# Linear attention with a two-layer feed-forward: seven products over pairs of chunks, with half of the middle results in DRAM

## The chip, the cores and the metric

The kernel runs on one core of a Trainium2 chip. The metric is device time in microseconds (us); the time of a kernel is the median of its runs.

## What is computed

```python
q_s = exp(q - max(q, axis=-1)); q_s = q_s / (sum(q_s, axis=-1) + 1e-9)   # q, k, v: 8 x 8 x 576 x 64
k_s = exp(k - max(k, axis=2));  k_s = k_s / (sum(k_s, axis=2) + 1e-9)
kv = einsum('bhsd,bhse->bhde', k_s, v)
x = einsum('bhsd,bhde->bhse', q_s, kv)        # as tokens: 4608 x 512
h = x @ w_in                                  # 512 x 2048
g = where(h >= 1, h, where(h <= -1, 0, (h + 1) ** 2 / 4))
out = g @ w_out                               # 2048 x 512
```

All is float32. Each large product is made of three matmuls over a high and a low part of its operands (high x low, high x high, low x high).

## The kernel before

The 4608 tokens are nine chunks (0 to 8) of T = 512. For each chunk, `attention(c, pr)` makes x in four pairs of heads: k's maximum (L693 to 696 on VectorE, L733 across partitions on GpSimd), subtraction L737, exponential L742, kv L752; q's softmax (L839 on GpSimd); the product x L896. The feed-forward then runs over NF = 16 blocks f of 128 middle columns. Its second layer is line L1330: for each f, four groups o of 3 matmuls of 512 columns into four PSUM banks o0 to o3, kept over all f.

The first layer has two forms. Chunks 0 to 2 (`PLAIN = 3`) use 12 matmuls h of 512 columns per f (L1169). Chunks 3 to 8 use seven products in place of eight (`PRODUCTS`, `two_first_layers`, L1226) over a 2 x 2 split: two f by the two halves of the chunk's 512 tokens. Each product is 6 matmuls of 256 columns; they build up in the banks hA, hb and hC, with copies sn (L364) and additions (L1250) between them, and leave four results of 128 x 256, which are those of f and f + 1 for all 512 tokens. Sums of weights are made in chunks 1 and 2 (`again`, L528 to L568), kept in DRAM and streamed back for each pair of f (`stream`). The sums of x are made once per chunk in xc (L931) and split into high and low parts (L937, L945).

After the first layer come, per f of 512 tokens: r (L1305, L1308 on ACT), the minimum (L1311 on VectorE), gh (L1315 on ACT) and gl (L1319 on VectorE). Then o can run. All of these have 128 x 512 elements.

The order of work on each engine is made by a planner. `Plan.op` records an operation with its engine, estimated duration, due time and the operations it needs; `Ring` says when a buffer comes free; `order` lists the operations by start and due times; `settle` improves the first part of that list by a search. The list is then issued as it stands, so each engine works through its own in order and a waiting instruction holds up all that stands behind it on its engine. SP issues every DMA.

## Time and profile before

| | |
|---|---|
| runs | 868.08, 863.57, 862.73 us; median 863.57 |
| profiled execution | 868.35 us, of which span 866.2 |
| TensorE (PE) | busy 850.4 us (98%), 5256 matmul instructions |
| VectorE (DVE) | 606.9 us (70%) |
| ScalarE (ACT) | 493.2 us (57%) |
| GpSimd (POOL) | 153.7 us (18%) |
| DMA | 179.09 MB, mean 207 GB/s |

The profile shows one execution. Busy time of an engine is the union of its instructions' spans. The chain is the work that ended last, followed back from the last instruction to what released each step. A row of a group reads: line, engine, operation, output <- inputs, shape, count | busy time, mean ns of one | idle time of the engine ahead of them and what ended it.

### The profile page before, as it was taken

The page shows a single profiled execution, that of the slowest core. Times are in us where ns is not written, and L with a number is a line of the kernel's source. Part 1 is how long each engine was busy: PE and PEld are TensorE (multiplying, and loading weights), DVE is VectorE, ACT ScalarE, POOL GpSimd, SP SyncE. Part 2 cuts the span into 40 slices and gives each one's busy share as a digit, 9 for nine tenths or more (in the row PEclk, how much of TensorE's full clock was granted, in tenths as well). Part 3 has the DMA queues.
Part 4 walks back from the last instruction along what each step waited for, and adds up shares of the span by engine and source line. Part 5 has one row for each costly group of instructions (what it writes and reads, how often), then busy time and mean ns, then how long its engine had stood idle before and what let it go on. Part 6 is the DMA issues. An engine that isn't in the chain of part 4 may idle for free.

```text
span 866.2 us, 14457 instructions
## 1 busy us (share of the span) xinstructions
PE 850.4 (98%) x5256; PEld 733.5 (85%) x5256; DVE 606.9 (70%) x1369; ACT 493.2 (57%) x909; POOL 153.7 (18%) x148
## 2 busy tenths in 40 slices
PE   8999899999999999999899999999999999999998
PEld 6788788888888888888788889889888888888886
DVE  7877777858777788887677787877676764343332
ACT  7887765544556465565456654566554564454444
POOL 5555442111113111112010111110111100000000
PEclk9999999999999999999999999999999999999999
DMA  9989776644755577655656475556554354445431
GB/s 329 292 284 303 252 255 225 213 142 162 247 187 171 194 257 265 217 184 194 222 183 226 175 264 183 212 184 233 198 194 176 133 203 179 177 165 209 183 146 48
DMA packets 47447, 179.09 MB, mean 207 GB/s; under 512 B 5265, under 2 KB 5521, under 8 KB 41233
## 3 DMA queue, kind: packets, MB, share of 16 engines
q1 hardware_dynamic: 47376, 178.18, 58.6%
q8 instruction: 41, 0.67, 0.3%
q14 instruction: 30, 0.24, 0.1%
HBM read 151.95 MB, written 26.21 MB: 206 GB/s over the span
## 4 chain that ended last, share of the span: by engine, by line
PE 89%; DMA 5%; DVE 3%; ACT 1%; issue 1%; POOL 0%; DVEq 0%; POOLq 0%; ACTq 0%
PE o L1330 42%; PE hA L1226 16%; PE h L1169 13%; PE hC L1226 8%; PE hb L1226 4%; PE x L896 3%; DMA st<-in_w 2%; PE kv L752 2%; DMA out<-osb 2%; PE warm L1469 1%; DMA k<-in_kt 1%; DVE hC L1250 1%; DVE st L438 0%; DVE st L441 0%; PE ep L713 0%
## 5 line engine op out<-in xcount | busy, mean ns | idle before, releaser
L1330 PE MATMUL o<-wl,gh 128*128 128x512 f32 x576 | 227.9, 396 | 1.4 <-DVE osb L366 1.3
L1330 PE MATMUL o<-wh,gh 128*128 128x512 f32 x576 | 225.9, 392 | 0.0
L1330 PE MATMUL o<-wh,gl 128*128 128x512 f32 x576 | 225.1, 391 | 0.1
L1226 PE MATMUL hA<-x,w 128*128 128x256 f32 x1152 | 173.6, 287 | 0.9 <-DVE hA L1250 0.5
L1226 PEld LDWEIGHTS hA<-x,w 128*128 128x128 f32 x1152 | 155.5, 190 | 19.4 <-DVE hA L1250 11.1
L1169 PE MATMUL h<-x,w 128*128 128x512 f32 x576 | 144.1, 395 | 0.3 <-DVE x L920 0.3
L1330 PEld LDWEIGHTS o<-wh,gl 128*128 128x128 f32 x576 | 108.3, 188 | 25.1 <-DVE gl L1319 1.3
L1169 PEld LDWEIGHTS h<-x,w 128*128 128x128 f32 x576 | 108.0, 189 | 23.7 <-DVE x L920 1.0
L1330 PEld LDWEIGHTS o<-wl,gh 128*128 128x128 f32 x576 | 108.7, 189 | 19.9 <-DVE osb L366 2.4
L1330 PEld LDWEIGHTS o<-wh,gh 128*128 128x128 f32 x576 | 108.8, 189 | 15.1
L1308 ACT ACTIVATE r<-r 128x512 f32<-128x512 f32 x144 | 91.4, 635 | 3.5
L1226 PE MATMUL hC<-x,w 128*128 128x256 f32 x576 | 85.7, 285 | 3.4 <-DVE gl L1319 3.4
L364 ACT COPY sn<-hA 128x256 f32<-128x256 f32 x87 | 32.5, 373 | 97.6 <-PE hA L1226 97.6
L1226 PEld LDWEIGHTS hC<-x,w 128*128 128x128 f32 x576 | 76.0, 192 | 3.8 <-DVE gl L1319 3.6
L1250 DVE TENSOR_TENSOR hC<-hb,sn 128x256 f32<-128x256 f32 x48 | 20.8, 432 | 81.3 <-PE hC L1226 80.5
L839 POOL TENSOR_TENSOR q<-q,qrz 128x512 f32<-128x512 f32 x36 | 38.2, 1063 | 199.1 <-DVE qrz L861 69.4
L1305 ACT ACTIVATE r<-h,half 128x512 f32<-128x512 f32 x48 | 33.1, 689 | 63.1 <-PE h L1169 62.8
L1305 ACT ACTIVATE r<-hC,half 128x512 f32<-128x512 f32 x48 | 33.1, 690 | 57.3 <-DVE hC L1250 57.3
L1311 DVE SCALAR_TENSOR_TENSOR h<-h,r 128x512 f32<-128x512 f32 x48 | 33.4, 697 | 35.0 <-ACT r L1308 34.7
L839 POOL TENSOR_TENSOR q<-q,qm 128x512 f32<-128x512 f32 x36 | 39.7, 1107 | 75.2 <-DVE qm L819 32.5
L733 POOL PARTITION_ALL_REDUCE m<-m x24 | 18.2, 760 | 195.5 <-DVE m L696 81.1
L1305 ACT ACTIVATE r<-hA,half 128x512 f32<-128x512 f32 x48 | 33.1, 690 | 22.3 <-PE hA L1226 20.1
...
## 6 DMA issues: line engine op xcount, KB each, us to landing
...
q<-in_q SPq DMA_DIRECT2D x36, 256.0 KB, 3.3
out<-osb SPq DMA_DIRECT2D x35, 256.0 KB, 3.9
```

Of the source, the lines that this page charges most:

```text
L364: nc.scalar.copy(out, src)
L733: nc.gpsimd.partition_all_reduce(t["mb"], t["m1"], P, bass_isa.ReduceOp.max)
L752: nc.tensor.matmul(t["kv"][d, :], t["k"][r, j, d], t["v"][r, j, i * (D + 1) : (i + 1) * (D + 1)], start=(j == 0), stop=(j == KJ - 1), tile ...
L839: nc.gpsimd.tensor_tensor(t["qf"], t["qf"], at, alu)
L896: nc.tensor.matmul(t["x"][:, :, p0:p1], lhs, rhs[:, :, p0:p1], start=(i == 0), stop=(i == 2),)
L1169: nc.tensor.matmul(t["h"], lhs, rhs, start=(at == 0 and i == 0), stop=(at == NPAIR - 1 and i == 2),)
L1226: nc.tensor.matmul(where(b), lhs, rhs, start=(begins and not kk and not m), stop=(ends and kk == 1 and m == 2), skip_group_check=True,)
L1250: nc.vector.tensor_tensor(out(), a(), b(), ALU.add)
L1305: nc.scalar.activation(t["r"], t["h"], AF.Relu, bias=half[:, :1], scale=0.5)
L1308: nc.scalar.activation(t["r"], t["r"], AF.Square)
L1311: nc.vector.scalar_tensor_tensor(t["h"], t["h"], 1.0, t["r"], ALU.max, ALU.min)
L1330: nc.tensor.matmul(outs[c, j], lhs[:, s], rhs, start=(f == 0 and i == 0), stop=(f == NF - 1 and i == 2),)
```

## The change

The seven products now go over pairs of chunks, (3, 4), (5, 6) and (7, 8): the 2 x 2 split is two f by two chunks, and each product is 6 matmuls of 512 columns. x of these chunks is written to DRAM (`xo`, `xkept`) and read back into xc, where `x_sums` makes the sums; the high and low parts lie in 14 places x0 to x13, of which chunks 0, 1 and 2 use x0 to x3, x4 to x7 and x10 to x13. The first chunk of a pair goes through the second layer between the products, as before. The second chunk's g (c12 and c22) goes through one of `NGS = 3` rooms gs to DRAM (`keep`), and is read back (`recall`) after the last products of the pair, when 16 f of o alone are run. Weights and their sums share `NWS = 5` rooms. The low parts of x and of a kept g, and the sums, can run on GpSimd or VectorE; `RELUCTANT = 3.0` is added to GpSimd's estimate when the planner chooses. For chunks 2 to 4 (`KM = 5`) k's maximum across partitions is made by a TensorE transpose, a VectorE reduction and a second transpose that spreads it, into the PSUM bank a.

```diff
-    ("P1", "A", 0, A11, B11),
-    ("P2", "B", 0, A12, B21),
-    ("P5", "C", 0, S1, T1),
-    ("P6", "A", 1, S2, T2),
-    ("P3", "C", 0, S4, B22),
-    ("P7", "A", 1, S3, T3),
-    ("P4", "A", 1, A22, T4),
+    ("P1", "A", "B11"),
+    ("P2", "B", "B21"),
+    ("P5", "C", "T1"),
+    ("P6", "A", "T2"),
+    ("P3", "C", "B22"),
+    ("P7", "A", "T3"),
+    ("P4", "A", "T4"),
...
+NWS, NGS = 5, 3
...
+KM = 5
...
-                        w[0] == e or t + us <= start(w[0], op, w[2]) + w[1]
+                        w[0] == e
+                        or t + us + self.bias(op, e) <= start(w[0], op, w[2]) + w[1] + self.bias(op, w[0])
...
                 km = do("DVE", 1.0, 0, k_max, lk, *rm.wait(), port=True)
                 rm.take(km)
 
-                mb = do("POOL", 13.6, 0.1, k_all, km, made[NF - 1, 1])
-                ks = do("DVE", 0.81, 2.5, k_sub, mb, port=True)
-                rm.free(ks)
+                if c < KM:
+                    rb = room("ps a", 1)
+                    tr = do("PE", 0.25, 0.5, k_tr, km, *rb.wait())
+                    rb.take(tr)
+                    kx = do("DVE", 0.25, 1, k_top, tr)
+                    rm.free(kx)
+                    mb = do("PE", 0.25, 1.5, k_spread, kx)
+                    ks = do("DVE", 0.81, 2.5, k_sub, mb)
+                    rb.free(ks)
+                else:
+                    mb = do("POOL", 13.6, 0.1, k_all, km, made[NF - 1, 1])
+                    ks = do("DVE", 0.81, 2.5, k_sub, mb, port=True)
+                    rm.free(ks)
...
-        rxc = room("xc", 1)
-        xo = do("ACT", 0.59, 5, x_out, xm, *(() if hi_half else rxc.wait()), other=[("DVE", 0.69, False)])
+        rxo = room("xo", 1)
+        xo = do("ACT", 0.59, 5, x_out, xm, *rxo.wait(), other=[("DVE", 0.69, False)])
+        rxo.take(xo)
         freed.free(xo)
...
-        xdone[c, kk] = done
+        xkept[c, pr] = dp.tile([P, T], F32, name=f"xk{c}_{pr}")
+        xdone[c, pr] = plan.save(0.45, at(5.2), x_store, [xo], 256)
+        rxo.free(xdone[c, pr])
...
+        for at, (cc, pr) in enumerate(((c, lo), (c + 1, lo), (c + 1, hi), (c, hi))):
+
+            def load(at=at, cc=cc, pr=pr):
+                if not at:
+                    t["xc"] = rp.tile([P, 5, T], F32, tag="xc", name=f"xc_{c}_{kk}", bufs=1)
+                nc.sync.dma_start(t["xc"][:, at, :], xkept[cc, pr])
...
+        def split(part, at, *deps):
+            place = 2 * PARTS.index(part) + kk
+            rx = ring(f"x{place}", 1)
...
+            def high():
+                xs[c, kk, part] = x_room(place)
+                nc.scalar.copy(xs[c, kk, part][:, 0, :], t["xc"][:, at, :])
+
+            def low(engine):
+                eng = nc.vector if engine == "DVE" else nc.gpsimd
+                x = xs[c, kk, part]
+                eng.tensor_tensor(x[:, 1, :], t["xc"][:, at, :], f32(x[:, 0, :]), ALU.subtract)
+
+            h = op("ACT", 0.59, due, high, [*deps, *rx.wait()])
+            rx.take(h)
+            done = either(0.69, low, h)
+            xdone[c, kk, part] = done
+            dones.append(done)
+            return done
...
+        b11 = split("B11", 0, loads[0])
+        t1 = either(0.69, comb(4, 1, 0), loads[0], loads[1])
+        t3 = either(0.69, comb(1, 2, 1), loads[2], t1)
+        t1s = split("T1", 4, t1)
+        b22 = split("B22", 2, loads[2])
+        t2 = either(0.69, comb(0, 2, 4), loads[2], t1, b11)
+        b21 = split("B21", 3, loads[3])
+        split("T3", 1, t3)
+        split("T2", 0, t2)
+        t4 = either(0.69, comb(3, 3, 0), t2, b21)
+        split("T4", 3, t4)
+        rxc.free(*dones)
...
+        def spilled(t, name):
+            def tile():
+                t["h"] = rp.tile([P, T], F32, tag="gs", name=f"{name}_{n}", bufs=NGS)
+                return t["h"]
+
+            return tile
...
+            deps = [loads[k // 2], xdone[c, 0, part], xdone[c, 1, part], *deps]
+            return op("PE", 1.36, due, product(k, begins, ends), deps)
...
-        c11 = dve(c_lo, lambda: where("B"), lambda: side["P1"], due + 0.6, p2, k1, p3)
-        rb.free(c11)
-        c12 = dve(c_hi, c_hi, lambda: side["U2"], due + 0.6, p3, u2)
-        p7 = mm(5, due + 1.0, u2, p6)
-        c22 = dve(a_hi, a_lo, lambda: side["P5"], due + 1.0, p7, k5)
-        rs.free(c11, c12, c22)
-        p4 = mm(6, due + 1.5, c22, p7)
...
+        c11 = dve(h["B"], h["B"], lambda: side["P1"], due + 2.8, p2, k1)
...
+        o12 = dve(spilled(c12, "c12"), h["C"], lambda: side["U2"], due + 8.4, p3, u2, *rgs.wait())
+        rgs.take(o12)
+        rc.free(o12)
+        rs.free(c11, o12)
+        p7 = mm(5, due + 10, u2, p6)
+        o22 = dve(spilled(c22, "c22"), h["A"], lambda: side["P5"], due + 11.4, p7, k5, *rgs.wait())
+        rgs.take(o22)
+        rs.free(o22)
+        p4 = mm(6, due + 12, o22, p7)
+        for mm_ in (p2, p6, p7, p4):
+            rws.free(mm_)
...
+            for name, last in zip(PRODUCTS, (p1, p2, p5, p6, p3, p7, p4)):
+                for kk in range(2):
+                    ring(f"x{2 * PARTS.index(name[2]) + kk}", 1).free(last)
+        return (banks["B"], [c11]), (banks["A"], [p4]), (c12, [o12]), (c22, [o22])
...
+        rr = ring("r", NR)
+        a = op("ACT", 0.69, due, g_relu, [*ready, *rr.wait()])
+        rr.take(a)
+        b = op("ACT", 0.63, due, g_square, [a])
+        d = op("DVE", 0.69, due, g_min, [b], port=kept)
+        rr.free(d)
+        return d
...
+    def keep(c, f, due, t, d):
+
+        def store():
+            nc.sync.dma_start(gkept[f], t["h"])
+
+        o = plan.save(0.45, due, store, [d], 256)
+        ring("gs", NGS).free(o)
+        made["g", c, f] = o
...
+    def recall(c, f, due):
+        t = {}
+
+        def load():
+            t["h"] = rp.tile([P, T], F32, tag="gs", name=f"gs_{c}_{f}", bufs=NGS)
+            nc.sync.dma_start(t["h"], gkept[f])
+
+        rgs = ring("gs", NGS)
+        o = op("SP", 0.45, due - 8, load, [made["g", c, f], *rgs.wait()], kb=256)
+        rgs.take(o)
+        return t, o
...
-        def g_lo():
+        def g_lo(engine="DVE"):
+            eng = nc.vector if engine == "DVE" else nc.gpsimd
             t["gl"] = gp.tile([P, T], F32R, tag="gl", name=f"gl_{n}")
-            nc.vector.tensor_tensor(t["gl"], t["h"], f32(t["gh"]), ALU.subtract)
+            eng.tensor_tensor(t["gl"], t["h"], f32(t["gh"]), ALU.subtract)
...
-        e = op("ACT", 0.62, due + 0.6 * STEP, g_hi, [d, *rg.wait()])
+        rg = ring("g", 2)
+        e = op("ACT", 0.62, due - 4, g_hi, [d, *rg.wait()])
         rg.take(e)
-        g = op("DVE", 0.69, due + 0.6 * STEP, g_lo, [e])
+        if kept:
+            ways = [("DVE", 0.69, True)]
+            g = op("POOL", 1.31, due - 2, g_lo, [e], port=True, other=ways)
+        else:
+            g = op("DVE", 0.69, due - 2, g_lo, [e])
...
-            else:
-                one, two = two_first_layers(c, p, due)
-                gs = [unit(c, 2 * p, due + 0.5 * STEP, *one), unit(c, 2 * p + 1, due + STEP, *two)]
-                rh.free(gs[1])
-                rh.free(gs[0])
...
+    for turn, c in enumerate(range(PLAIN, NCHUNK, 2)):
+        begin = START + STEP * NF * PLAIN + turn * LONG
+        prepare_two(c, begin)
+        for kk in range(2):
+            x_sums(c, kk, begin - (28, 10)[kk])
+        step = LONG / 11
+        for p in range(NF // 2):
+            due = begin + step * p
+            one, two, three, four = two_first_layers(c, p, due)
+            f = 2 * p
+            d = middle(c, f, due + 6, *one)
+            ring("ps b", 1).free(second_layer(c, f, due + 13, one[0], d))
+            d = middle(c + 1, f, due + 11, *three, kept=True)
+            keep(c + 1, f, due + 13, three[0], d)
+            d = middle(c + 1, f + 1, due + 15, *four, kept=True)
+            keep(c + 1, f + 1, due + 17, four[0], d)
+            d = middle(c, f + 1, due + 16, *two)
+            ring(f"ps h{p % 2}", 1).free(second_layer(c, f + 1, due + 20, two[0], d))
+        for f in range(NF):
+            due = begin + step * 8 + step * 3 / NF * f
+            t, d = recall(c + 1, f, due)
+            ring("gs", NGS).free(second_layer(c + 1, f, due + 4, t, d, kept=True))
```

Three places of the order. TensorE, in chunk 7 (of before: the last three of the seven products of p = 3, with o of f 4 and 5; o_7_j is the output for token block j, wh, wl the weights, gh, gl the two parts of g):

```order
L1226 MATMUL hC_7_3_8097<-x_7_0_6888,w0_7_3_7915 128x256 x3
L1226 MATMUL hC_7_3_8097<-x_7_1_7595,w0_7_3_7915 128x256 x3
L1330 MATMUL o_7_3_7910<-wl4_105,gh_7_4_8060 128x512
L1330 MATMUL o_7_3_7910<-wh4_104,gh_7_4_8060 128x512
L1330 MATMUL o_7_3_7910<-wh4_104,gl_7_4_8066 128x512
L1226 MATMUL hA_7_3_8090<-x_7_0_6888,w1_7_3_7950 128x256 x3
L1226 MATMUL hA_7_3_8090<-x_7_1_7595,w1_7_3_7950 128x256 x3
L1330 MATMUL o_7_0_7840<-wl5_107,gh_7_5_8079 128x512
L1330 MATMUL o_7_0_7840<-wh5_106,gh_7_5_8079 128x512
L1330 MATMUL o_7_0_7840<-wh5_106,gl_7_5_8084 128x512
L1226 MATMUL hA_7_3_8090<-x_7_0_6888,w1_7_3_7950 128x256 x3
L1226 MATMUL hA_7_3_8090<-x_7_1_7595,w1_7_3_7950 128x256 x3
```

And of the changed kernel, the last o of f 5, two more products, f 6's first two groups and P4 (the first four products of this p stand ahead of f 5):

```order
L1439 MATMUL o_7_3_7473<-wh5_106,gl_7_5_7726 128x512
L1292 MATMUL hC_7_3_7739<-x4_6920,w_7_3_2_7634 128x512 x3
L1292 MATMUL hC_7_3_7739<-x5_7273,w_7_3_2_7634 128x512 x3
L1292 MATMUL hA_7_3_7707<-x10_6914,w_7_3_2_7634 128x512 x3
L1292 MATMUL hA_7_3_7707<-x11_7350,w_7_3_2_7634 128x512 x3
L1439 MATMUL o_7_0_7439<-wl6_109,gh_7_6_7759 128x512
L1439 MATMUL o_7_0_7439<-wh6_108,gh_7_6_7759 128x512
L1439 MATMUL o_7_0_7439<-wh6_108,gl_7_6_7764 128x512
L1439 MATMUL o_7_1_7447<-wl6_109,gh_7_6_7759 128x512
L1439 MATMUL o_7_1_7447<-wh6_108,gh_7_6_7759 128x512
L1439 MATMUL o_7_1_7447<-wh6_108,gl_7_6_7764 128x512
L1292 MATMUL hA_7_3_7707<-x12_6977,w_7_3_3_7677 128x512 x3
```

Between the fourth product and the fifth stand the 12 matmuls of f 5 now, and between the sixth and the seventh two groups of o instead of one.

ACT at the end of chunk 2 (gh and r of f 12 to 14, the copies of the next chunk's x, the split of weight sums w). Before:

```order
L1315 CAST gh_2_12_3203<-h_2_12_3164 128x512
L364 COPY xc_3_1_3208<-x_3_2_3182 128x512
L880 CAST qh_3_3_3226<-tp_3_3_3210 128x512
L1305 ACTIVATE r_2_13_3241<-h_2_13_3212,half_93 128x512
L1308 ACTIVATE r_2_13_3241<-r_2_13_3241 128x512
L742 ACTIVATE k_4_0_2632<-k_4_0_2632 128x640
L1315 CAST gh_2_13_3274<-h_2_13_3212 128x512
L364 COPY xc_3_1_3208<-x_3_3_3260 128x512
L563 CAST w0_2_7_3140<-ss_7_3216 128x2x256
L937 CAST x_3_1_3297<-xc_3_1_3208 128x256
L563 CAST w1_2_7_3145<-ss_7_3216 128x2x256
L1305 ACTIVATE r_2_14_3309<-h_2_14_3281,half_93 128x512
```

After:

```order
L379 COPY xo_4_2_3664<-x_4_2_3640 128x512
L1170 CAST x10_3674<-xc_3_0_2609 128x512
L1170 CAST x12_3683<-xc_3_0_2609 128x512
L591 CAST w_s_7_1_3686<-ss_7_3576 128x2x256
L785 ACTIVATE k_5_0_2826<-k_5_0_2826 128x640
L379 COPY xo_4_3_3740<-x_4_3_3715 128x512
L1381 ACTIVATE r_2_13_3748<-h_2_13_3692,half_93 128x512
L1384 ACTIVATE r_2_13_3748<-r_2_13_3748 128x512
L1170 CAST x1_3758<-xc_3_1_3713 128x512
L1423 CAST gh_2_13_3766<-h_2_13_3692 128x512
```

Between gh_2_12 and r_2_13 now stand the casts into x10 and x12, which had been chunk 2's x, and between r_2_13 and gh_2_13 the cast into x1 from xc_3_1.

SP, around the first load of k for chunk 2 (st are weights from the input, s and b their split parts written to DRAM, w_1_0 and w_1_1 their first fetches). Before:

```order
L426 DMA st15_1_1354<-in_w 128x1024
L493 DMA s0_7_119<-w0_0_7_1313 128x1024
L509 DMA w0_1_0_1367<-s0_0_112 128x1024
L509 DMA w1_1_0_1372<-s1_0_120 128x1024
L659 DMA k_2_0_1381<-in_k 128x640
L493 DMA s1_7_127<-w1_0_7_1356 128x1024
L659 DMA k_2_2_1396<-in_k 128x640
L659 DMA k_2_1_1423<-in_k 128x640
```

After:

```order
L442 DMA st15_1_1335<-in_w 128x1024
L508 DMA b14_126<-w_0_14_1311 128x1024
L690 DMA k_2_2_1367<-in_k 128x640
L508 DMA b15_127<-w_0_15_1359 128x1024
L516 DMA w_1_0_1399<-b0_112 128x1024
L516 DMA w_1_1_1425<-b1_113 128x1024
L690 DMA k_2_3_1430<-in_k 128x640
L690 DMA k_2_0_1452<-in_k 128x640
L690 DMA k_2_1_1490<-in_k 128x640
```

k_2_0's load was ahead of the write of the last weight (s1_7) and is now behind it (b15) and behind two fetches. Its maximum is needed on TensorE by the transpose mt_2_0, between two groups of o of f 13:

```order
L1240 MATMUL h_0_14_1486<-x3_489,w_0_14_1311 128x512 x3
L1439 MATMUL o_0_2_572<-wl13_1028,gh_0_13_1470 128x512
L1439 MATMUL o_0_2_572<-wh13_1027,gh_0_13_1470 128x512
L1439 MATMUL o_0_2_572<-wh13_1027,gl_0_13_1492 128x512
L765 MATMUL mt_2_0_1527<-ident_95,m2_2_0_1501 128x128
L1439 MATMUL o_0_0_604<-wl13_1028,gh_0_13_1470 128x512
L1439 MATMUL o_0_0_604<-wh13_1027,gh_0_13_1470 128x512
L1439 MATMUL o_0_0_604<-wh13_1027,gl_0_13_1492 128x512
L915 MATMUL tp_1_3_1537<-ident_95,q_1_3_1006 128x128 x4
```

The transpose L765 is new there; before, TensorE had nothing of chunk 2 at this place.

More of the change, by code (lines that the diff above doesn't have):

```diff
@@ L211, in early @@
             for d in op.deps:
-                if d.engine == op.engine == "SP":
+                if d.engine == op.engine == "SP" and not d.store:
                     at = max(at, d.start + 0.45)
@@ L245, in settle, with bias @@
         return order
+    def bias(self, op, engine):
+        return self.RELUCTANT if op.engine == "POOL" != engine else 0.0
     def inherit(self):
@@ L309, in order @@
                 hop = self.HOP + u.slack if (u.engine != e or len(u.ways) > 1) else 0.0
-                at = free["SP"] if u.engine == e == "SP" else end + hop
+                at = free["SP"] if u.engine == e == "SP" and not op.store else end + hop
                 u.ready = max(u.ready, at)
@@ L475, in weights @@
         rs.free(d)
-        room = ring(f"ws{odd}", 2)
         e = op(
@@ L481, in weights @@
             high,
-            [d] + (early_users if f >= NF - LATE and half else []) + ([] if half else room.wait()),
+            [d] + (early_users if f >= NF - LATE and half else []) + ([] if half else rws.wait()),
         )
@@ L546, in do @@
         def do(us, emit, *deps):
[L547 to L548 removed]
+            return op(
+                "POOL",
+                1.85 * us,
+                due + 0.5 * STEP,
+                emit,
+                deps,
+                port=True,
+                other=[("DVE", us, True)],
+            )
         w0 = do(0.69, whole(0), made[c, 2 * p], *waits)
@@ L1083, in attention @@
             kvread[c - 1, pr] = xm
-        rx = room(f"x{kk}", 2)
         freed = rpk if first else rpq
         if c < PLAIN:
-            waits = [xfirst[c, kk]] if hi_half else rx.wait()
-            xh = do("ACT", 0.59, 5, x_hi, xm, *waits)
-            if not hi_half:
-                rx.take(xh)
-                xfirst[c, kk] = xh
+            rx = room(f"x{PLACES[c] + pr}", 1)
+            xh = do("ACT", 0.59, 5, x_hi, xm, *rx.wait())
+            rx.take(xh)
             xdone[c, pr] = do("DVE", 0.69, 5.2, x_lo, xh)
@@ L1115, in attention @@
-        o13 = comb(0.69, 5.1, slice(4, 8, 2), slice(1, 4, 2), slice(0, 2), *both)
-        o2 = comb(0.42, 5.2, 5, 3, 4, o13)
-        o4 = comb(0.42, 5.3, 7, 2, 5, o2)
-        parts = ((slice(2, 8), slice(1, 7), 1.45, 1.77, (o13, o2, o4)), (0, 0, 0.37, 0.42, both))
-        done, waits = [], rx.wait()
-        for at_, to, hus, lus, deps in parts:
-            hi, lo = x_split(at_, to)
-            xh = do("ACT", hus, 5.4, hi, *deps, *waits)
-            done.append(do("DVE", lus, 5.5, lo, xh, port=True))
-            if len(done) == 1:
-                rx.take(xh)
@@ L1126, in attention, with x_sums, either, comb @@
-        rxc.free(*done)
-        xdone[c, kk] = done
+        xkept[c, pr] = dp.tile([P, T], F32, name=f"xk{c}_{pr}")
+        xdone[c, pr] = plan.save(0.45, at(5.2), x_store, [xo], 256)
+        rxo.free(xdone[c, pr])
+    def x_sums(c, kk, due):
+        t = {}
+        rxc = ring("xc", 1)
+        lo, hi = 2 * kk, 2 * kk + 1
+        loads = {}
+        waits = rxc.wait()
+        for at, (cc, pr) in enumerate(((c, lo), (c + 1, lo), (c + 1, hi), (c, hi))):
[3 more added lines that the diff above has]
+                nc.sync.dma_start(t["xc"][:, at, :], xkept[cc, pr])
+            prev = loads.get(0)
+            loads[at] = op("SP", 0.45, due - 8, load, [xdone[cc, pr], prev, *waits], kb=256)
+            if not at:
+                rxc.take(loads[0])
+        def either(us, emit, *deps):
+            other = [("DVE", us, True)]
+            return op("POOL", 1.85 * us, due, emit, deps, port=True, other=other)
+        def comb(to, a, b):
+            def emit(engine):
+                eng = nc.vector if engine == "DVE" else nc.gpsimd
+                xc = t["xc"]
+                eng.tensor_tensor(xc[:, to, :], xc[:, a, :], xc[:, b, :], ALU.subtract)
+            return emit
+        dones = []
+        def split(part, at, *deps):
[26 more added lines that the diff above has]
+        rxc.free(*dones)
@@ L1267, in copy @@
-            return op("ACT", 0.38, due, snap(name, b), deps, other=ways)
+            ways = [("DVE", 0.69, False)]
+            return op("ACT", 0.6, due, snap(name, b), deps, other=ways)
         def dve(out, a, b, due, *deps):
-            return op("DVE", 0.42, due, add(out, a, b), deps)
-        p1 = mm(0, due, *rh.wait())
-        rh.take(p1)
+            return op("DVE", 0.69, due, add(out, a, b), deps)
+        h = {k: (lambda k=k: banks[k]["h"]) for k in banks}
+        p1 = mm(0, due, *ra.wait())
@@ L1295, in two_first_layers @@
-        if p == NF // 2 - 1:
-            for kk in range(2):
-                ring(f"x{kk}", 2).free(p4, p3)
-        return (tt["C"], [c11, c12]), (tt["A"], [c22, p4])
-    def unit(c, f, due, t, ready):
+        p5 = mm(2, due + 2.8, *rc.wait())
+        rc.take(p5)
+        c11 = dve(h["B"], h["B"], lambda: side["P1"], due + 2.8, p2, k1)
+        k5 = copy("P5", "C", due + 4.2, p5, *rs.wait())
+        rs.take(k5)
+        p6 = mm(3, due + 5, k1, p1)
+        u2 = copy("U2", "A", due + 6.4, p6)
```

348 lines of the change are left out of this document (168 added, 180 removed).

## The prediction

> **What bounds the kernel now.** I read the busy shares first, then the chain that ended last, then that chain through one regular stretch, then the windows around the places where it is not regular. The first line gives each engine's busy time; the next two say which engine and lines make up the chain.
>
> ```profile
> PE 850.4 (98%) x5256; PEld 733.5 (85%) x5256; DVE 606.9 (70%) x1369; ACT 493.2 (57%) x909; POOL 153.7 (18%) x148
> PE 89%; DMA 5%; DVE 3%; ACT 1%; issue 1%; POOL 0%; DVEq 0%; POOLq 0%; ACTq 0%
> ```
>
> TensorE (PE) is busy 98% of the span and carries 89% of the chain, so a change counts by what it does to TensorE's instruction stream and to the few places where that stream stands still. The windows give, per stretch, each engine's busy time, the granted clock, the DMA share and GB/s.
>
> ```profile
> 290.00:385.00 95.00, 94.93 (x629) 83.69 (x627) 78.24 (x185) 55.45 (x102) 15.46 (x16) 1.00 0.62 222
> 395.00:426.00 31.00, 27.53 (x193) 23.76 (x192) 21.90 (x55) 16.05 (x30) 3.29 (x4) 0.94 0.63 209
> 736.50:747.12 10.62, 10.62 (x67) 9.43 (x67) 3.99 (x8) 4.73 (x9) 0.00 (x0) 1.00 0.45 173
> ```
>
> The third row is one regular round of a late chunk: both layers of a pair of f for 512 tokens, 10.62 us without a gap. The first row shows the same fullness around the end of chunk 2. The second has a hole. Here is TensorE's timeline there (start, duration, instruction, and in brackets the idle time before it).
>
> ```profile
> 416.19 0.89 PE L1226 MATMUL hA<-x,w 128*128 128x256 f32 x6
> 420.48 1.65 PE L1226 MATMUL hC<-x,w 128*128 128x256 f32 x6 [3.40 <-DVE gl L1319]
> 421.93 1.48 PE L1226 MATMUL hA<-x,w 128*128 128x256 f32 x6
> 423.21 1.04 PE L1226 MATMUL hC<-x,w 128*128 128x256 f32 x6
> ```
>
> **The change part by part.** The profiled execution took 868.35 us (span 866.2 and 2.15 around it), 4.8 above the median of the three runs, 863.57. I sum differences against the profiled execution and apply the sum to the median.
>
> *The products.* These are the chain's pieces of that round (start, duration, instructions), and after them two pieces of chunk 1 whose matmuls have 512 columns.
>
> ```profile
> 736.50 2.07 PE o L1330 x9
> 738.56 0.71 PE hb L1226 x6
> ...
> 742.06 0.72 PE hC L1226 x6
> ...
> 746.31 0.81 PE hA L1226 x6
> ...
> 172.19 2.72 PE h L1169 x12
> 174.91 2.72 PE o L1330 x12
> ```
>
> A 512-column matmul costs 2.72/12 = 226.7 ns, a 256-column one 0.7165/6 = 119.4 ns (mean of the undisturbed products, 0.71 to 0.72), so two narrow ones cost 238.8, 12.1 more than a wide one. The change replaces 2016 narrow by 1008 wide: 2016 x 119.4 - 1008 x 226.7 = 12.2 us. The rest comes from waits: a round of two chunks takes 2 x 10.62 = 21.24 now and should take 7 products x 1.36 + 16 groups of o x 0.68 = 20.40 when nothing waits. For 24 pairs of f that is **-20.2**. The P4 now starts 0.10 late (0.81 for 0.71): its addition lasts 0.43 and has 0.69 of o as cover, so the way from TensorE to VectorE and back costs 0.69 + 0.10 - 0.43 = 0.36. In the new rounds of chunk 7 two groups of o, 1.36, stand between P7 and P4, against an addition of 512 columns of 0.69 (gl's row, below) + 0.36 = 1.05: covered. At worst the 0.84 per round shrinks to the 0.51 of the matmuls alone, -12.2; at best -20.2, which I take, since the order shows the covers.
>
> The Trainium skill's page "TensorE: Matmul & The Clock Gate", section "Back-to-back issue gap", gives an isolated gap of N/2.4 + 2.5 ns, which speaks against this change: 215.8 and 109.2 ns, so that 12.2 would be 2.6 and the whole term about -10.5. Both rows above stand beyond it (226.7 and 119.4), and their step from 256 to 512 columns, 107.3, is about its 106.7; what differs is the fixed part, 12 against 2.5, which is what the change saves.
>
> *The hole at 416.* The chain puts it down to one write of a result.
>
> ```profile
> 411.92 7.28 DMA out<-osb
> ```
>
> ACT stood behind a copy that waited for this write, gh and gl came late, TensorE stood 3.40 and then ran three products at a lower clock (1.65, 1.48 and 1.04 where starts are 0.72 apart elsewhere): 3.40 + 1.6 = **-5.0**. In the new order this place has other neighbours; I credit this hole and none of the small losses at the other chunk ends. From nothing to -5.0.
>
> The same page's "Part 1: The HAM clock gate" says that after an idle window of about 3.4 us the array runs at half rate until it has been busy as long; 1.65 after 3.40 agrees. A hole of that length costs half as much again.
>
> *k's maximum.* Chunks 2 to 4 get 24 transposes of 128 columns, chained through a reduction on VectorE. The nearest are these (four of 128 columns, then what started next):
>
> ```profile
> 105.77 0.60 PE L713 MATMUL ep<-ident,k 128*128 128x128 f32 x4
> 106.13 1.63 PE L1169 MATMUL h<-x,w 128*128 128x512 f32 x6
> 109.64 0.27 PE L722 MATMUL et<-ident,k 128*64 128x128 f32 x1
> ```
>
> Four start within 0.36, 0.09 each; the whole duration of a lone one is 0.27. So 2.2 to 6.5 us; they stand alone among other matmuls, I take 0.15: **+3.6**. GpSimd's reduction that goes (L733) is not among the chain's lines.
>
> *A transpose that waits for k (chunk 0 to 1).* SP now issues in_k of the first pair of chunk 2 behind the write of b15 and two fetches, where it stood ahead of the last write. That write waits for the low part of the last weight, which ends at 109.67 in the first row of its kind below, and in_k then lands and is reduced:
>
> ```profile
> k<-in_k SPq DMA_DIRECT2D x24, 320.0 KB, 5.5
> 108.35 1.32 POOL L464 TENSOR_TENSOR w<-st,w 128x512 fp32r<-128x512 f32 x1 [2.24 <-ACT w L460]
> L693 DVE TENSOR_TENSOR m<-k 128x256 f32<-128x256 f32 x24 | 12.3, 511 | 2.0 <-DMA k<-in_k 1.6
> L695 DVE TENSOR_TENSOR m<-m 128x128 f32<-128x128 f32 x24 | 8.5, 355 | 0.8
> L696 DVE TENSOR_TENSOR m<-m,k 128x128 f32<-128x128 f32 x24 | 7.8, 323 | 0.8
> ```
>
> From the end of that low part: up to five issues, 0 to 0.45 each (the planner's spacing), 5.5 to landing, 1.19 of maximum: 7 to 9 us. TensorE has 12 o of f 12, kv, the 12 matmuls of h_0_14 and 3 o of f 13 ahead of the transpose mt_2_0: 2.72 + 2.72 + 0.68 and a little for kv, some 6.4, if it has got no further by then. The rows behind mt_2_0 on TensorE need nothing of it, but the queue is in order. Between 0 and 5; I take **+2.4**.
>
> *The end of chunk 2.* The x places x10 to x13 are chunk 2's, whose last reader in the new order is h_2_14 (TensorE runs 15 before 13 and 14). ACT's casts into x10 and x12 wait for it and stand ahead of r_2_13, and the cast into x1 behind them waits for xc_3_1, loaded into the one room xc that the low parts of x10 and x12 free. gh_2_13 comes after all of them. The pieces:
>
> ```profile
> q<-in_q SPq DMA_DIRECT2D x36, 256.0 KB, 3.3
> L364 ACT COPY xc<-x 128x512 f32<-128x512 f32 x20 | 11.8, 591 | 3.5 <-PE x L896 2.7 <-DVE x L941 0.6
> L1315 ACT CAST gh<-h 128x512 fp32r<-128x512 f32 x48 | 28.2, 587 | 24.7 <-DVE h L1311 24.0 <-PE x L896 0.3
> L1319 DVE TENSOR_TENSOR gl<-h,gh 128x512 fp32r<-128x512 f32 x48 | 33.0, 688 | 5.9 <-ACT gh L1315 4.4
> ```
>
> From the middle of h_2_14: a way of 0.2, cast 0.59, low part 0.69, load of 256 KB 3.3, then cast 0.59, gh 0.59, gl 0.69, and ways: 6.9 to 7.2, of which TensorE fills 1.36 with the rest of h_2_14. It stands about 5.2, and by the hole above pays a third of that again at the lower clock: **+6.9**. Nothing if casts and loads run ahead of TensorE; 9 if the load takes in_k's 5.5.
>
> *The first pair.* Some rounds of chunk 3 have only one group of o (0.68) or a product's rest between P5 and P3 or P6 and P7, where a copy needs 0.59 + 0.36 = 0.95: 0.27 in four or five places, **+1.2** (0 to 3). The end of each pair's interleaved part has the last f's middle, r 0.69 and 0.64, minimum 0.70, gh, gl and the ways, 3.8, behind 3.4 of work: 0.4 x 3 = **+1.2**. VectorE gets the reductions and wide additions with the attention of chunks 5 and 6: its instructions between the first and last product of this pair sum to 113 us, by their rows' means, in about 124 of TensorE (91%, against 78.24/95 = 82% in the first window row). Some groups will be late; I take **+1.5**, from 0 to the 5.0 of one hole.
>
> *The kept halves.* Their 16 f per pair have only o, 2.72 each. The low parts run on GpSimd, behind q and xc work:
>
> ```profile
> L464 POOL TENSOR_TENSOR w<-st,w x16: 1291/1316/1694, 19.7 to 108.3; 128x512 fp32r<-128x512 f32 x16
> L839 POOL TENSOR_TENSOR q<-q,qm x36: 1040/1052/1624, 5.1 to 688.4; 128x512 f32<-128x512 f32 x36
> ```
>
> A low part of 1.32 fits twice into 2.72. Between gl_6_3 and gl_6_4 stand q (1.05) and a sum (about 1.3): 1.32 x 2 + 2.4 against two f, 5.44; where VectorE holds its port longer, something slips. **+1.5** for three phases (0 to 5).
>
> The sum is -20.2 - 5.0 + 3.6 + 2.4 + 6.9 + 1.2 + 1.2 + 1.5 + 1.5 = **-6.9**: 868.35 to 861.4 in a profiled execution, and 863.57 to **856.7**.
>
> **The rivals.** *The two waits of TensorE are hidden.* If ACT is ahead of TensorE at the end of chunk 2 and SP ahead at its start, 2.4 + 6.9 go, and the time is 847 (842 to 851). For it: SP's transfers land faster when little else moves. Against it: the casts wait for h_2_14 itself, which TensorE cannot run earlier.
>
> *VectorE is overfull in the first pair.* At 91% one or two groups as late as the one at 420.48 give 5.0 each: 862 to 867, with a slipping order 872. For it: the second window's hole had VectorE at 21.90 of 31. Against it: the planner could move low parts to GpSimd.
>
> *The recall of kept g bounds the kept halves; this ends slower.* Three rooms gs hold a g from the issue of its load until its low part is done: landing L + gh 0.59 + low 1.32 + ways 0.15. Three rooms give 3 x 2.72 = 8.16, so it decides from L = 6.1 on. The median of 256 KB is 3.3, but the chain has a write of that size at 7.28. At 7.28 each f would take (9.34 - 8.16)/3 = 0.39 longer, 48 x 0.39 = 18.7: 875.
>
> *A wide matmul costs two narrow ones*, 238.8 ns. Then 12.2 of the first term is gone: 869. The two rows, 119.4 and 226.7, are of the same engine at the same clock, 1.00, and speak against it. The skill's gap would give 866.
>
> **How the numbers follow.** The forecast, 851 to 863, has 0.52; hidden waits 0.26; VectorE overfull 0.12; kept g 0.06; the wide matmul 0.04. One per cent, 8.6 us, is about what a measurement of this kernel can tell from no change. Faster by more means below 854.9: the hidden waits, and a quarter of the forecast, 0.14: 0.40. Slower by more means above 872.2: kept g, and a little of VectorE: 0.07. Within: 0.53. The range leaves out the lower part of the hidden waits (0.09), kept g and half of the overfull case above 869: 846 to 869.
>
> **What the changed profile would show.** Right: products of six in 1.36 without gaps in chunk 7's rounds; TensorE's matmuls down by 984; one idle piece of about 5 us near 300 us, released by gl of f 13 in chunk 2; a smaller one near 112 before a transpose; 43.5 us for each run of 16 f after a pair. Wrong: idle pieces in the runs of kept g released by DMA; products of 1.43; holes in the first pair released by VectorE; no hole near 300, by which the time would be 847.

## The result and the profile after

| | before | changed |
|---|---|---|
| median of 20 runs each, us | 866.16 (862.73 to 870.42) | 869.22 (866.11 to 871.97) |
| ratio | | 1.0034, 95% interval 1.0018 to 1.0050 |
| profiled execution, span | 868.35, 866.2 | 870.23, 868.5 |

The forecast was a gain of 6.9 us; the kernel lost about 3. The three runs that the prediction started from had a median 2.6 below that of the twenty, so in ratio it said 0.992 against 1.003. That the measured 869.22 is close to the 869 of the rival of the wide matmul is chance: its mechanism, 238.8 ns for a wide matmul, is not there. First, the page of the changed kernel: busy times, and its chain by engine and line.

```profile
PE 842.0 (97%) x4272; PEld 685.4 (79%) x4272; DVE 554.7 (64%) x1199; ACT 478.4 (55%) x842; POOL 298.3 (34%) x265
PE 80%; DVE 8%; DMA 7%; ACT 2%; POOL 2%; issue 2%; POOLq 0%; SPq 0%; DVEq 0%; ACTq 0%
```

TensorE has 984 matmuls fewer and is busy 8.4 us less, yet the span is 2.3 longer. Its share of the chain fell from 89% to 80%; VectorE, DMA and GpSimd took it. GpSimd's busy time nearly doubled. The windows show where: one round of two chunks, and two long stretches (before's first and second row behind them).

```profile
742.96:757.91 14.95, 14.95 (x67) 12.39 (x66) 7.53 (x11) 6.99 (x12) 0.00 (x0) 1.00 0.47 158
100.00:320.00 220.00, 214.33 (x1187) 173.64 (x1186) 173.69 (x407) 115.02 (x208) 101.98 (x97) 0.99 0.58 201
320.00:500.00 180.00, 169.90 (x872) 138.18 (x871) 132.61 (x302) 106.68 (x189) 46.07 (x40) 0.97 0.65 217
```

```profile
100.00:320.00 220.00, 220.00 (x1159) 183.34 (x1158) 171.95 (x389) 120.40 (x211) 45.96 (x45) 0.99 0.58 202
320.00:500.00 180.00, 176.35 (x1246) 156.21 (x1245) 140.36 (x339) 101.99 (x192) 26.73 (x27) 0.99 0.60 213
```

The round takes 14.95, and with the two kept f behind it 14.95 + 5.44 = 20.39, as forecast (20.40). What is lost lies between 100 and 500 us: TensorE was idle for 3.7 of these 400 us before and for 15.8 now, and GpSimd works 148 us there instead of 73. These are the largest idle pieces on TensorE's timeline of the changed kernel:

```profile
132.78 1.55 PE L1240 MATMUL h<-x,w 128*128 128x512 f32 x4 [2.37 <-DVE x L956]
329.53 0.79 PE L1439 MATMUL o<-wl,gh 128*128 128x512 f32 x1 [4.69 <-ACT gh L1423]
481.77 0.80 PE L1439 MATMUL o<-wl,gh 128*128 128x512 f32 x1 [3.09 <-ACT osb L379]
```

To compare stretches I sum, from the whole timeline, how much longer each matmul took from its start to the next one's than a plain rate (226.7 ns for 512 columns, 119.4 for 256, their undisturbed rates for the small ones, 0 for the new transposes). This counts waits, slow clock and transposes; the plain work itself fell by 12.2 us, as forecast: from three quarters of the changed kernel's wide products (L1292) it is 227 ns or less to the next matmul's start. In us lost, by stretch from the span's start:

| | 0-100 | 100-320 | 320-500 | 500-end |
|---|---|---|---|---|
| before | 12.7 | 3.4 | 10.7 | 9.6 |
| changed | 12.4 | 16.5 | 18.7 | 3.2 |

### The profile page after: what moved, and what is told of

Same layout as the page of the kernel before. It is cut to its first block, busy times and chain, and to the rows that moved or that the text cites. A ratio compares the mean times of both kernels' runs of the same rounds, so it can differ in the third digit from the quotient of the medians.

```text
span 868.5 us, 12535 instructions
## 1 busy us (share of the span) xinstructions
PE 842.0 (97%) x4272; PEld 685.4 (79%) x4272; DVE 554.7 (64%) x1199; ACT 478.4 (55%) x842; POOL 298.3 (34%) x265
## 4 chain that ended last, share of the span: by engine, by line
PE 80%; DVE 8%; DMA 7%; ACT 2%; POOL 2%; issue 2%; POOLq 0%; SPq 0%; DVEq 0%; ACTq 0%
PE o L1439 38%; PE hA L1292 14%; PE h L1240 10%; PE hC L1292 7%; PE hb L1292 3%; PE x L939 3%; DMA st<-in_w 2%; PE kv L795 2%; DMA out<-osb 1%; DMA k<-in_k 1%; DMA xk<-xo 1%; PE warm L1612 1%; DVE qrzo L861 1%; DVE gl L1428 1%; DVE m L726 1%
## 5 line engine op out<-in xcount | busy, mean ns | idle before, releaser
L1240 PE MATMUL h<-x,w 128*128 128x512 f32 x576 | 147.5, 399 | 4.1 <-DVE x L956 2.4
L1292 PE MATMUL hA<-x,w 128*128 128x512 f32 x576 | 147.3, 392 | 1.2 <-DVE c L1316 1.2
L1292 PEld LDWEIGHTS hA<-x,w 128*128 128x128 f32 x576 | 107.3, 188 | 24.8 <-DVE c L1316 2.0
L1428 POOL TENSOR_TENSOR gl<-gs,gh 128x512 fp32r<-128x512 f32 x39 | 50.3, 1291 | 165.7 <-PE o L1439 122.6
L1292 PE MATMUL hC<-x,w 128*128 128x512 f32 x288 | 73.8, 391 | 0.4 <-DVE gl L1428 0.3
L1423 ACT CAST gh<-gs 128x512 fp32r<-128x512 f32 x48 | 29.9, 622 | 72.9 <-PE o L1439 57.5
L1381 ACT ACTIVATE r<-c,half 128x512 f32<-128x512 f32 x48 | 34.7, 722 | 60.8 <-DVE c L1316 60.7
L1292 PEld LDWEIGHTS hC<-x,w 128*128 128x128 f32 x288 | 53.7, 188 | 13.1 <-DVE gl L1428 1.7
L1316 DVE TENSOR_TENSOR c<-hC,sn_P 128x512 f32<-128x512 f32 x24 | 16.6, 690 | 56.3 <-PE hC L1292 56.3
L1175 POOL TENSOR_TENSOR x<-xc,x 128x512 fp32r<-128x512 f32 x27 | 35.5, 1327 | 33.6 <-ACT x L1170 26.1
```

What stands on the lines that cost most here:

```text
L1175: eng.tensor_tensor(x[:, 1, :], t["xc"][:, at, :], f32(x[:, 0, :]), ALU.subtract)
L1240: nc.tensor.matmul(t["h"], lhs, rhs, start=(at == 0 and i == 0), stop=(at == NPAIR - 1 and i == 2),)
L1292: nc.tensor.matmul(banks[b]["h"], lhs, rhs, start=(begins and not kk and not m), stop=(ends and kk == 1 and m == 2), skip_group_check=True,)
L1381: nc.scalar.activation(t["r"], t["h"], AF.Relu, bias=half[:, :1], scale=0.5)
L1423: nc.scalar.copy(t["gh"], t["h"])
L1428: eng.tensor_tensor(t["gl"], t["h"], f32(t["gh"]), ALU.subtract)
```

## The experiments

Each kernel is the changed one with the edit shown (`...` where lines are left out), and each ratio is to the kernel before, timed on the same chip. Losses are those of one profiled execution, which lies up to 4.8 us off its kernel's median, so a few us between two kernels' losses tell nothing alone. Most of these edits also make the planner lay out the whole order anew, so more than the named place changes. The first question was whether the single holes are causes.

**Chunk 2's x in other places.**

```diff
-    PLACES = (0, 4, 10)
+    PLACES = ((0, 1, 2, 3), (4, 5, 6, 8), (7, 9, 11, 13))
...
```

> Chunk 1's x moves to places x4, x5, x6, x8 and chunk 2's to x7, x9, x11, x13, so that all first-half x sums of the first pair (even places) can be written while chunk 2 still runs. Theory A (the hole at the end of chunk 2, 7.4 us above the plain rate with its slow clock, comes from the casts into x10 and x12 that wait for chunk 2's last readers): the hole goes, ratio to before from 1.0034 to about 0.995 (862 us where before is 866). Rival (ACT is simply late there, or the wait moves to the casts into x7 to x13 and so to the third product): a hole of 4 us or more remains within the first two rounds, ratio 1.000 or more.

871.34 us, ratio 1.0046 (1.0024 to 1.0069). The hole at the end of chunk 2 is gone: 0.4 us lost between 320 and 350 instead of 9.2. The time did not fall: the ratio is the rival's, though the rival's hole in the first two rounds isn't there. TensorE's timeline of this kernel has others, further on:

```profile
414.10 2.93 PE L1292 MATMUL hA<-x,w 128*128 128x512 f32 x6 [3.78 <-DVE c L1316]
477.10 0.41 PE L939 MATMUL x<-qh,kvt 128*128 128x384 f32 x1 [3.12 <-DVE kvt L840]
```

**Two writes of chunk 3's output left out.**

```diff
-                nc.sync.dma_start(ov[j][:, s], t[i][:, s])
+                if c != PLAIN or j > 1:
+                    nc.sync.dma_start(ov[j][:, s], t[i][:, s])
```

> The writes of the first two output blocks of chunk 3 to DRAM are left out (the order stays the same, these 256 output rows are not produced). Theory B (the hole of 3.1 us at the switch from chunk 3 to the kept half of chunk 4, 4.8 with its slow clock, is the wait of the third and fourth copies of o for the two osb rooms, that is for a write that took 6.5 us): the hole goes, 4 to 5 us, ratio about 0.998. Rival (ACT or the low part of the first kept g holds TensorE there anyway): under 1.5 us, ratio 1.002 or more.

871.72 us, 1.0052 (1.0032 to 1.0071). The wait for the room is gone too, and 10 us later the first product of the next pair waits for its x instead. The ratio is the rival's again, by another wait than the rival's:

```profile
491.68 0.96 PE L1292 MATMUL hA<-x,w 128*128 128x512 f32 x3 [2.69 <-POOL x L1175]
```

**A third room for the copies of o** (`osb` with three buffers).

> A third room for the copies of o, order unchanged. Theory B: the third copy no longer waits, the fourth still waits for the first write; TensorE has one more group of o and some x of 0.7 us to run first, so the hole of 3.1 us falls to 1 to 2.5 and the slow clock with it may go: ratio 0.9995 to 1.002. Rival as for the left-out writes: no change, 1.0034.

868.97 us, 1.0021 (1.0005 to 1.0038). The hole at the switch fell from 3.1 to 1.3, and 0.85 came up behind it at the same product. The ratio is just above B's 0.9995 to 1.002, and its interval holds the 1.0034 of the changed kernel: no gain is shown.

**k's maximum by GpSimd again.**

```diff
-KM = 5
+KM = 2
```

> k's maximum across partitions by GpSimd for all chunks again; everything else as changed. Theory C (the transposes cost TensorE about 1 us themselves, but they draw chunk 2's maxima into the change from chunk 0 to 1, where VectorE is a chain without a gap from 112 to 133 us and TensorE loses 5.2 + 2.2 us): the losses there fall to 2 to 4, ratio about 0.998. Rival (GpSimd, now with the low parts, is then too late with q and x): holes released by GpSimd, ratio 1.005 or more. Second rival (nothing but the 24 transposes changes): 1.001 to 1.003.

915.73 us, 1.0576 (1.0540 to 1.0612). C was right about its place and wrong on the whole: only 5.1 us are lost between 100 and 320, but 58 between 320 and 500, where the first pair waits for x again and again (and 15 more than in the changed kernel ahead of 100 us):

```profile
347.24 1.65 PE L1292 MATMUL hA<-x,w 128*128 128x512 f32 x3 [3.37 <-POOL x L1175]
...
371.60 0.55 PE L939 MATMUL x<-qh,kvt 128*128 128x256 f32 x1 [4.20 <-DVE kvt L840]
...
384.50 1.65 PE L1292 MATMUL hC<-x,w 128*128 128x512 f32 x3 [6.52 <-DVE x L1175]
```

So the transposes can't simply be taken back: in this order the attention of chunks 3 and 4 comes too late.

**The planner told of all readers of a place.** A place of x is freed for the planner by f 15; TensorE runs 13 and 14 after it. (Here and in all later kernels the planner's `late` also falls back to an operation's earlier start where one that uses it isn't placed yet.)

```diff
...
+        readers[c, f] = prev
         if f == NF - 1:
             for pr in range(NPAIR):
-                ring(f"x{PLACES[c] + pr}", 1).free(prev)
+                ring(f"x{PLACES[c] + pr}", 1).free(*(readers[c, g] for g in range(NF - 4, NF)))
```

> The planner is told that the x places of a plain chunk are read by its last four f (it counted f 15 alone, while TensorE runs 15 before 13 and 14). Theory A1 (the hole at the end of chunk 2 comes from this blind spot, and taking it away is kept): losses between 320 and 350 us from 9.2 to under 3, ratio to before 0.995 to 0.998. Theory A2 (the stretch from there to 490 us is bound by another chain, the attention of chunks 4 to 6 on VectorE, ACT and the DMAs, so that holes come back in it, as when the places were changed): losses in 320 to 350 fall, those in 350 to 500 rise by as much, ratio 1.002 to 1.005.

869.19 us, 1.0022 (0.9996 to 1.0049). The hole at the end of chunk 2 is gone (1.0 lost between 320 and 350), and the stretch behind it rose, from 9.5 to 15.2 between 350 and 500, as A2 had it:

```profile
492.32 0.79 PE L1440 MATMUL o<-wh,gl 128*128 128x512 f32 x1 [5.00 <-POOL gl L1429]
```

**With that, k's maxima of chunk 2 later.**

```diff
+KLATE = 118.0
...
+                wait = (KLATE + 8 * pr) * (c == KT)
-                km = do("DVE", 1.0, 0, k_max, lk, *rm.wait(), port=True)
+                km = do("DVE", 1.0, 0, k_max, lk, *rm.wait(), port=True, late=wait)
```

> The same, and k's maxima of chunk 2 not before 20 to 45 us later, behind the change from chunk 0 to 1. Theory C1 (tying k's maximum to TensorE's queue there, with VectorE one chain from 112 to 133 us, costs 5 to 6 us): losses between 100 and 140 us from 8.2 to 2 to 3, ratio 0.005 to 0.007 below the kernel without it. Rival (VectorE is full there with chunk 1's q anyway): within 0.002 of it.

885.80 us, 1.0214 (1.0189 to 1.0239). The losses between 100 and 140 fell from 7.5 (free) to 0.6, and those between 320 and 500 rose from 16.2 to 31.3. C1 was right about the place and missed the time, and so did its rival: what was put off was missing later.

**Readers and third room; and all three.**

> The planner told of the readers, and a third room for the copies of o. By B: the wait for a write of o at the switch from chunk 3 to 4 falls by 1 to 2.5 us against the kernel without the room, ratio 0.001 to 0.003 lower; rival: the same, since the first products of the next pair wait for x just behind it.

868.84 us, 1.0012 (0.9983 to 1.0040): 0.001 below free, which the two intervals don't tell apart.

> All three. By A1, B and C1 together: ratio 0.987 to 0.992, faster than before. By A2: 0.996 to 1.000, since only the gain ahead of 320 us is kept.

883.35 us, 1.0197 (1.0178 to 1.0216): a miss, for the reason just seen.

By now the pattern was plain. Between 100 and 500 us the changed kernel loses 35.2 us; without the hole at chunk 2's end 33.8 (places) and 34.6 (free), with the third room 34.0, without two writes 31.9. Whichever wait was taken away, the sum stayed or fell by 3.3 at most (without two writes, from the fastest of that kernel's executions, 4.4 below its median), and none of these medians is told apart from the changed kernel's. Two theories remained: D, the attention is due too early, since both chunks of a pair need x before the pair's first product; E, the work that went to GpSimd is slow there and slows VectorE.

**The attention of chunk 4 left out.**

```diff
+            if cc == PLAIN + 1:
+                for k in range(2):
+                    xkept[cc, pr + k], xdone[cc, pr + k] = xkept[c, pr + k], xdone[c, pr + k]
+                continue
```

> The attention of chunk 4 is left out: its x is chunk 3's, read twice (so chunk 4's and the next batch's outputs are not the reference's). TensorE loses about 5 us of kv and x work with it. Theory D (both chunks of a pair need their x before the pair's first product, so the attention of chunk 4 must be done by 320 us instead of 410; VectorE, ACT and GpSimd cannot, and the 34 us that TensorE loses between 100 and 500 us keep their sum wherever a single wait is taken away): without these four units the losses between 100 and 500 fall to under 20, the time to 846 to 855, ratio 0.977 to 0.987. Rival E (the losses come from the order at single places and from GpSimd's work on VectorE's shared port): losses 28 to 34, time 862 to 865, ratio 0.995 to 0.999, by the 5 us alone.

Chunk 4's x is chunk 3's here. 850.15 us, 0.9805 (0.9749 to 0.9861), and 18.5 us lost between 100 and 500. As D expected.

**Five plain chunks, readers known.**

```diff
-PLAIN = 3
+PLAIN = 5
-    PLACES = (0, 4, 10)
+    PLACES = (0, 4, 10, 4, 10)
```

> Chunks 3 and 4 in the plain form too, pairs (5, 6) and (7, 8) by products, planner told of the readers. The plain form of a pair costs 8 rounds of 10.88 instead of 9.52: 10.9 us more. By D there are two more plain chunks of time for the attention that the pairs need early: losses between 100 and 500 fall from 34.6 to 15 to 20, so 860 to 866, ratio 0.993 to 0.999. By E the losses stay: 878 to 882, ratio 1.014 to 1.018.

855.32 us, 0.9866 (0.9820 to 0.9911): 5 us below the least that D expected, and far from E's 1.014. The losses between 100 and 500 are 10.1, less than before the change. Its window shows a TensorE without a gap:

```profile
320.00:500.00 180.00, 180.00 (x982) 149.24 (x981) 118.24 (x302) 89.59 (x160) 29.94 (x31) 1.00 0.51 167
```

**Reluctance 0, readers known.**

```diff
-    RELUCTANT = 3.0
+    RELUCTANT = 0.0
```

> The planner's reluctance to take work from GpSimd set to 0, planner told of the readers: 139 instead of 252 elementwise operations on GpSimd, the rest on VectorE. Theory E (GpSimd's work slows VectorE on the shared port: the small copies of 32 rows take 275 instead of 190 ns between 100 and 320 us, k's second maximum 618 instead of 362, some 16 us in all): losses between 100 and 500 from 34.6 to 20 to 28, ratio 0.988 to 0.996. Rival D (VectorE's time is what is short): VectorE gets 113 operations of 0.4 to 0.7 us more, losses rise to 40 or more, ratio 1.006 or more.

857.32 us, 0.9889 (0.9843 to 0.9936); 19.5 us lost between 100 and 500. As E expected; D in the form that VectorE's time is what is short expected 1.006 or more, and that form is refuted. The windows, and the groups of VectorE in the whole kernel, of this kernel and then of the changed one:

```profile
100.00:320.00 220.00, 216.30 (x1207) 176.04 (x1206) 190.97 (x463) 120.66 (x217) 70.57 (x63) 1.00 0.62 209
320.00:500.00 180.00, 177.45 (x923) 144.72 (x922) 141.14 (x317) 107.16 (x189) 25.34 (x25) 1.00 0.68 222
L861 DVE COPY qrzo<-qz 32x16 f32<-32x16 f32 x112 | 23.3, 208 | 2.0
L724 DVE TENSOR_TENSOR m<-k 128x256 f32<-128x256 f32 x24 | 14.1, 589 | 0.3
L1175 DVE TENSOR_TENSOR x<-xc,x 128x512 fp32r<-128x512 f32 x37 | 24.9, 695 | 0.6 <-ACT x L1170 0.5
```

```profile
L861 DVE COPY qrzo<-qz 32x16 f32<-32x16 f32 x112 | 28.3, 253 | 2.0
L724 DVE TENSOR_TENSOR m<-k 128x256 f32<-128x256 f32 x24 | 17.8, 742 | 3.8 <-DMA k<-in_k 3.6
L545 POOL TENSOR_TENSOR sw<-w 128x512 f32<-128x512 f32 x14 | 18.0, 1291 | 20.9 <-DMA w<-b 10.7 <-DVE z L810 6.1 <-DVE qmo L861 4.1
L1175 POOL TENSOR_TENSOR x<-xc,x 128x512 fp32r<-128x512 f32 x27 | 35.5, 1327 | 33.6 <-ACT x L1170 26.1
```

VectorE is busier by 26 us in these 400 us and TensorE stands 9.5 less. A low part of x takes 0.70 on VectorE and 1.33 on GpSimd, and the small copies and k's maxima on VectorE got faster with GpSimd's share halved (253 to 208 ns, 742 to 589).

Do the three runs tell D from E? From the whole timelines I sum how much longer VectorE's instructions between 100 and 500 us that start while GpSimd works took than the median of the same line, tiles and shape elsewhere:

| | before | changed | chunk 4 left out | five plain | reluctance 0 and readers | maxima by GpSimd |
|---|---|---|---|---|---|---|
| VectorE longer beside GpSimd, us | 17.0 | 35.8 | 19.7 | 18.3 | 24.5 | 21.4 |
| TensorE's loss there, us | 14.1 | 35.2 | 18.5 | 10.1 | 19.5 | 63 |

It fell in D's two kernels as well; without chunk 4's attention GpSimd was as busy in this stretch as in the changed kernel (147.8 us against 148.1), and yet it held up VectorE by half as much. So D's runs don't leave E out. Nor is this time all: with k's maxima by GpSimd it is low and the loss the largest. No run here moves the due times and leaves the work as it is.

**Reluctance 0 alone.**

> The changed kernel with the planner's reluctance to take work from GpSimd at 0 and nothing else: half of GpSimd's additions and subtractions go to VectorE. If that choice alone made the change lose, ratio 0.985 to 0.992 and losses between 100 and 500 us under 22, though TensorE's readers of the x places stay unknown to the planner. If it needs the readers too: the hole at the end of chunk 2 stays (7 us), ratio 0.994 to 1.000.

864.32 us, 0.9975 (0.9956 to 0.9993). It needs the readers too: the hole at the end of chunk 2 is still there (3.99 idle, released by gh), and with it 7 of the 864. So the knowledge of the readers, worth nothing while the stretch was short of attention (free), is worth 7 us once it is not.

**The best versions.** Third room, reluctance 0 and readers, with three and with five plain chunks.

> Readers known, reluctance 0, third room for the copies of o: against the kernel without the room (0.9889) the hole of 1.9 at the switch from chunk 3 to 4 goes: 0.986 to 0.989. If holes there only move: 0.989 to 0.991.

855.78 us, 0.9870 (0.9845 to 0.9894), not told apart from the kernel without the room.

> Five plain chunks, readers known, reluctance 0, third room. If compression (D) and GpSimd (E) are two sides of one shortage, five plain chunks have already removed it and reluctance 0 adds nothing: 0.985 to 0.988. If they add: losses between 100 and 500 from 10 to 6, 0.981 to 0.984.

854.59 us, 0.9863 (0.9835 to 0.9891), not told apart from five plain chunks alone: what five plain chunks and reluctance 0 relieve overlaps, as its expectation had it for one shortage seen from two sides. Either version beats both kernels by over 1%.

## Why the prediction was wrong, by its own steps

| step | forecast | measured in the profiles |
|---|---|---|
| matmuls, 2016 narrow to 1008 wide | -12.2 | -12.2 |
| waits in the rounds, with the first pair, the ends and the kept halves (350-460 without the hole, and 500-end) | -8.0 + 5.4 | 13.0 to 7.4: -5.6 |
| the hole at 416 | -5.0 | -5.0 there, and +3.9 in 460-500 |
| transposes and the wait for in_k (100-320) | +3.6 + 2.4 | 3.4 to 16.5: +13.1 |
| end of chunk 2 (320-350) | +6.9 | 1.0 to 9.2: +8.2 |
| 0-100 | 0 | -0.3 |
| sum | -6.9 | +2.1 |

**The products** were right to 0.1 us, and so was the round. The gap of N/2.4 + 2.5, by which only 2.5 would have been saved (the 2.6 comes of rounded gaps), did not hold, nor did the rival of the wide matmul.

**The end of chunk 2** was right in its chain and nearly in its size (4.69 idle and 3.5 of slow clock, 8.2 in all; 5.2 and 1.7, 6.9, forecast). TensorE was released by gh, one step ahead of the gl that was named. The chain:

```profile
322.12 1.37 PE h L1240 x6
...
323.51 0.63 ACT x L1170
...
324.17 1.22 DVE x L1175
...
325.44 2.56 DMA xc<-xk
...
328.02 0.32 ACT x L1170
```

Its size is no proof that it made the kernel slow: taking it away gained nothing until the shortage behind it was gone.

**The hole at 416** is the first step that failed. It was credited because its neighbours change. But its cause, a write of o that blocks a room, was not changed: the chain of the changed kernel has it again at the next such place.

```profile
474.55 6.50 DMA out<-osb
481.05 0.02 issue
481.07 0.02 ACTq L379
481.09 0.04 issue
481.13 0.59 ACT osb L379
```

The write took 6.50 (7.28 before), ACT copied only then, and TensorE, which in the kept half has little but o, waited for the bank. At 660.46 it stood 0.85 more behind a write of 6.29. Here the way to look is not whether the row moves but whether the mechanism is still in the program.

**The change from chunk 0 to 1** is the second; its row has the largest error, 13.1 against 6.0. The prediction counted how long in_k would be late and how much TensorE had to do meanwhile; mt_2_0 itself waited 0.3 or less, and there is no hole of the kind that was forecast near 112. The 24 transposes, +3.6 in the sum, took 0.9 from their starts to the next ones', and 1.8 was lost right ahead of them. The prediction did not follow VectorE, where chunk 2's maxima now stand among chunk 1's own work: three sets of them in 15 us. Before, VectorE had the first set there and the second 17 us later:

```profile
116.42 0.76 DVE L693 TENSOR_TENSOR m<-k 128x256 f32<-128x256 f32 x1 [1.61 <-DMA k<-in_k]
133.76 0.43 DVE L693 TENSOR_TENSOR m<-k 128x256 f32<-128x256 f32 x1
```

The chain of the changed kernel runs through VectorE almost without a gap from 112 to 133 us:

```profile
112.06 1.41 DVE m L724
...
113.50 0.72 DVE m L726
...
114.24 0.78 DVE m L727
...
119.04 0.81 DVE m L724
...
119.87 0.30 DVE m L726
...
120.20 0.29 DVE m L727
...
124.16 0.34 DVE m L724
...
124.53 1.03 DVE m L726
...
125.58 1.28 DVE m L727
```

and the x of chunk 1 that ends the wait of 2.37 comes last (L956). Four of these rows lie under GpSimd's, from the timeline of GpSimd at that place:

```profile
113.26 0.80 POOL L559 TENSOR_TENSOR ss<-sw 128x256 f32<-128x256 f32 x1
114.14 0.74 POOL L559 TENSOR_TENSOR ss<-ss,sw 128x256 f32<-128x256 f32 x1
124.09 1.30 POOL L882 TENSOR_TENSOR q<-q,qm 128x512 f32<-128x512 f32 x1 [4.54 <-DVE qm L862]
125.36 1.35 POOL L596 TENSOR_TENSOR w_s<-ss,w_s 128x512 fp32r<-128x512 f32 x1
```

L726 and L727 take 0.30 and 0.29 at 119.87 and 120.20, where GpSimd stands. The four others take 0.72, 0.78, 1.03 and 1.28, and each ends 0.15 after the GpSimd instruction that had started ahead of it. So it is in the whole trace: of the 48 instructions of these two lines ten start under a GpSimd instruction and end 0.15 after it, and the 38 others take 0.29. The Trainium skill's page "SBUF — State Buffer", section "SBUF: two separate sides", says that a VectorE instruction with two SBUF inputs and a GpSimd instruction that reads SBUF hold the shared pair of ports one at a time, and that the second waits for the first to finish. The ends of the ten agree with it; no run here takes the port alone away.

By the same sums this place is only half of the row of 13.1: some 6.4 of it lie between 100 and 140 us, 6.6 between 140 and 320. The second half is many small pieces, with no idle time over 1.0 us among them; what each waits for stays open.

**What the prediction had no step for** is that the attention is due earlier and that more of the work goes to GpSimd. It summed waits at places. The pairing makes chunk 4's x due with chunk 3's, one chunk earlier, while sums and low parts went to an engine at half the speed. One reduction of q per pair of heads (L830 before, L873 now) counts the attention that VectorE does between 100 and 320 us, ten pairs before and fourteen now:

```profile
L830 DVE TENSOR_REDUCE qm<-q 128x16 f32<-128x512 f32 x10 | 6.7, 668 | 0.0
L873 DVE TENSOR_REDUCE qm<-q 128x16 f32<-128x512 f32 x14 | 9.3, 665 | 0.0
```

Leaving chunk 4's attention out, giving it two more chunks, and taking work off GpSimd each removed 15 to 25 of the 35 us. That the stretch is short of what the attention and GpSimd's work need is shown by these runs; that the due time and not the amount of work is what counts is argued. The rival of a full VectorE was near it, but took fullness from a count of busy time in the first pair (91%); the window of 100 us there has 73 busy, and at reluctance 0 VectorE had 26 us more to do and the kernel was faster: what was late were chains through several queues, not a full engine. The rival also put it behind chunk 2's end; nearly half of the loss (16.5 of 35.2) was ahead of it.

**Kept g** was no bound: no idle piece over 0.3 us is released by a load of g, whose 256 KB landed in 2.6 us (median). **One sentence ahead of the prediction is wrong**: RELUCTANT is added to VectorE's estimate for work that is GpSimd's by default, so it keeps work on GpSimd; it was read the other way, and so a cost that a single number sets was not weighed.

What stays open: how much is the due time and how much GpSimd, and of the latter how much is its own slowness and how much the port. VectorE's 18.8 us more beside GpSimd is VectorE's time, and no run says how much of it reached TensorE.
